# Attention stage of a fused kernel: the first inputs begun in order, the later ones as one transfer

## The chip, the cores and the metric

The kernel runs on one core of a Trainium2 chip. The metric is device time in microseconds (us) from launch to end; for one core it is the time of that core. The engines named below are TensorE (PE: matrix products, with PEld for its weight loads), VectorE (DVE), ScalarE (ACT), GpSimd (POOL) and SyncE (SP, which here only issues transfers, "DMA"s). ACT and POOL can issue transfers too. A transfer issued by SP stands in SP's queue, one issued by ACT in ACT's queue; sixteen DMA engines work off the packets of all queues. Shapes are written partitions x elements.

## The reference, cut to what matters

All arithmetic is in float32. The first half is a causal weighted sum over 7 neighbouring tokens for each of 8 heads, the second a mixture of experts in which each token goes to one expert by a greedy assignment with a capacity.

```python
B, S, D = 8, 3584, 192          # 28672 tokens; 8 heads of 24 columns, 7 weights each
w = softmax(weight, axis=-1)
x_pad = concat([zeros(B, 6, D), x], axis=1)
attn[b, s, h] = sum(w[h, k] * x_pad[b, s + k, h] for k in range(7))

logits = attn @ w_gate          # [28672, 8]
for idx in argsort(-logits.flatten()):      # greedy, capacity 3584 tokens an expert
    ...
out[mask_e] = relu(attn[mask_e] @ w1[e]) @ w2[e]        # 192 -> 1024 -> 192
```

## The kernel before, in words

**Two stages.** Stage 1 (from the start to about 164 us) computes `attn`, writes it to memory, and finds the assignment. Stage 2 (from there to the end) gathers each expert's tokens and applies its two matrices; there TensorE works nearly without a gap.

**Stage 1, tiles.** The 28672 tokens are 16 tiles (`NHB`) of 1792 tokens, two to a sequence. `load(i)` brings tile i into `X`, [118 partitions x 16 x 192]: 112 partitions (`W`) each hold one token of 16 windows, and the 6 partitions ahead of them, the halo, hold the 6 tokens before each window. So a load is a small transfer for the halo (line 189 in even tiles, 192 in odd ones) and two transfers of half of the 112 partitions' data each (line 194, windows 0 to 7 and 8 to 15). The first half is issued by SP, the second by ACT; for tile 0 both are issued by SP.

**conv(i)** takes one matrix product per head: `TH` (the 7 weights laid out as a 118 x 112 band, made by `toeplitz`) times X, in four PE instructions a head, into the PSUM tile `cv`; ACT then copies `cv` into the output tile `a` (an "evacuation"). `mid(h)`, called between the product and its evacuation, does other work: transposes of the previous tile's `a` (`aT`, DVE), the gate products (`pl`, `pt` on PE, with the gate matrix `GF`, which is the tile named `c_mu`), and steps of the assignment (`bg`), whose pace is set by a hand-kept model of engine time. After the eighth head ACT issues the store of `a` to `attn` (line 208, 1344 KB). For tile 14 the store is held back until head 2 of tile 15 (line 1631).

**What sets the order.** Each engine works its instructions in the order in which the program writes them. X has four buffers, so `load(i + 3)`, written ahead of `conv(i)`, waits until the PE instructions of `conv(i - 1)` are over; `a` has three buffers. `cv` has four. In the main loop (`for i in range(NHB)`) SP's issues are therefore halo, first half of tile i + 3, once a tile, and ACT's issues are the second half of tile i + 3 ahead of the eight evacuations of tile i, and the store behind them. Each transfer of SP and ACT reports on one of eight completion semaphores (DMAHW0 to DMAHW7), taken in turn; an engine that issues a transfer first waits until the transfer that used the same semaphore last has landed.

**The start.** `load(0)`, then `toeplitz`, in which `load(1)` stands behind the exponential, then `gate_ops`: four transfers of the gate matrix into the four 32-partition quarters of `wgr` (line 169), POOL's clearing of `GF` and its four copies of `wgr` into it (line 173), and two small DVE instructions on `pi`, made from a POOL instruction that stands behind those copies. Then `load(2)`, then the loop with `load(3)`.

**The end of stage 1.** At tile 13 the program issues the raw weights of the first expert (`wload`, lines 1229 to 1234, tiles `raw`) on SP, behind the load of tile 15. Inside `conv(13)` ACT rounds four of them to the type that the products of stage 2 need (`w<-raw`), each between two evacuations.

Of the kernel before, what the change touches and what calls it, by code (L numbers as in the profile page):

```python
# [6 lines left out]
F32 = mybir.dt.float32  # L7
# [8 lines left out]
NE, D, NTOK, F, CAP = 8, 192, 28672, 1024, 3584  # L16
W, HW_, NHB = 112, 16, 16
# [97 lines left out]
def build(ctx, tc, nc, x, weight, wg, attn, LT, wk):  # L115

    k = K()
    k.nc = nc
    k.tc = tc
    V, A, PE, P = nc.vector, nc.scalar, nc.tensor, nc.gpsimd  # L120
    cst = ctx.enter_context(tc.tile_pool(name="cst", bufs=1, side="right"))


    wb = cst.tile([128, 8, 7], F32, name="wb")
    nc.sync.dma_start(wb, bass.AP(tensor=weight.tensor, offset=weight.offset, ap=[[0, 128], [7, 8], [1, 7]]))
    pmi = cst.tile([128, 128], I32, name="pmi")
    P.iota(pmi, pattern=[[-1, 128]], base=0, channel_multiplier=1)
    D0 = cst.tile([128, 128], BF, name="D0")
    V.tensor_copy(D0, pmi)
    TH = cst.tile([128, 8, 128], F32, name="TH")  # L130
    P.memset(TH[:, :, W:128], 0.0)
    MK = cst.tile([128, 7, W], BF, name="MK")
    for j in range(7):
        V.tensor_scalar(MK[:, j], D0[:, 0:W], float(j), None, op0=OP.is_equal)
    wm = cst.tile([128, 8], F32, name="wm")

    def toeplitz():
        V.tensor_reduce(wm, wb, axis=AX.X, op=OP.max)
        V.tensor_tensor(wb, wb, wm[:, :, None].to_broadcast([128, 8, 7]), op=OP.subtract)
        A.activation(wb, wb, AF.Exp)  # L140
        load(1)
        V.tensor_reduce(wm, wb, axis=AX.X, op=OP.add)
        V.tensor_scalar(wm, wm, 1e-9, None, op0=OP.add)
        V.reciprocal(wm, wm)
        V.tensor_tensor(wb, wb, wm[:, :, None].to_broadcast([128, 8, 7]), op=OP.mult)

        tk = cst.tile([128, 2, W], F32, name="tk")
        for h in (1, 5):
            A.activation(TH[:, h, 0:W], MK[:, 0], AF.Copy, scale=wb[:, h, 0:1])
            for j in range(1, 7):  # L150
                A.activation(tk[:, j % 2], MK[:, j], AF.Copy, scale=wb[:, h, j:j + 1])
                P.tensor_tensor(TH[:, h, 0:W], TH[:, h, 0:W], tk[:, j % 2], op=OP.add)
        for hs in ((0, 2), (3, 4), (6, 7)):
            for j in range(7):
                for h in hs:
                    t = TH[:, h, 0:W]
                    if j == 0:
                        V.tensor_scalar(t, MK[:, 0], wb[:, h, 0:1], None, op0=OP.mult)
                    else:
                        V.scalar_tensor_tensor(t, MK[:, j], wb[:, h, j:j + 1], t, op0=OP.mult, op1=OP.add)  # L160


    wgr = cst.tile([128, 6, 8], F32, name="wgr")
    GF = wk.tile([128, 6, 32], F32, name="c_mu")
    pm = wk.tile([128, 1], F32, name="pm")

    def gate_ops():
        for pb in range(4):
            nc.sync.dma_start(wgr[32 * pb:32 * pb + 32], wg.rearrange("(c f) e -> f c e", f=32))
        P.memset(GF, 0.0)  # L170
        for pb in range(4):
            q = slice(32 * pb, 32 * pb + 32)
            P.tensor_copy(GF[q, :, 8 * pb:8 * pb + 8], wgr[q])

        pi = cst.tile([128, 1], I32, name="pi")
        P.iota(pi, pattern=[[0, 1]], base=0, channel_multiplier=1)
        V.tensor_scalar(pi, pi, 24, None, op0=OP.bitwise_and)
        V.tensor_scalar(pm, pi, 24.0, -1.0, op0=OP.is_equal, op1=OP.mult)


    X, AT, AA = {}, {}, {}

    def load(i):
        t = X[i] = k.xp[i % 4].tile([118, 16, D], F32, name="X")
        b, hf = divmod(i, 2)
        o = x.offset + (b * 3584 + hf * 1792) * D
        if hf == 0:
            P.memset(t[0:6, 0], 0.0)
            nc.sync.dma_start(t[0:6, 1:16], bass.AP(tensor=x.tensor, offset=o + (W - 6) * D,
                                                    ap=[[D, 6], [W * D, 15], [1, D]]))  # L190
        else:
            nc.sync.dma_start(t[0:6], bass.AP(tensor=x.tensor, offset=o - 6 * D, ap=[[D, 6], [W * D, 16], [1, D]]))
        for eng, w in ((nc.sync, 0), (A if i else nc.sync, 8)):
            eng.dma_start(t[6:118, w:w + 8], bass.AP(tensor=x.tensor, offset=o + w * W * D, ap=[[D, W], [W * D, 8], [1, D]]))

    def conv(i, mid, hold=None):
        t = X.pop(i)
        a = AA[i] = k.ap[i % 3].tile([128, 16, D], F32, name="a")
        o = a.rearrange("p w (h c) -> p h w c", c=24)
        for h in range(8):  # L200
            ps = k.cps.tile([128, 512], F32, name="cv")
            PE.matmul(ps[:, 0:384], TH[0:118, h], t[:, :, h * 24:(h + 1) * 24], start=True, stop=True)
            mid(h)
            A.activation(o[:, h], ps[:, 0:384].rearrange("p (w c) -> p w c", c=24), AF.Copy)
        put = partial(A.dma_start, attn[i * 1792:(i + 1) * 1792].rearrange("(g p b) d -> p g (b d)", g=4, b=4),
                      a[0:W].rearrange("p (g b) d -> p g (b d)", b=4))
        if hold is None:
            put()
        else:
            hold.append(put)  # L210

    def transp(i, u):

        if u == 0:
            AT[i] = [k.hp[i % 2].tile([128, 16, 6, 32], F32, name="aT")]
        V.transpose(AT[i][0][:, 4 * u:4 * u + 4].rearrange("p w c t -> p (w c t)"),
                    AA[i][:, 4 * u:4 * u + 4].rearrange("p w d -> p (w d)"))
        if u == 3:
            AA.pop(i)

    def logits(i, u):

        if u == 0:
            AT[i].append(k.bank("pl"))
        pl = AT[i][-1]
        for c in range(4):
            w = slice(4 * c, 4 * c + 4)
            PE.matmul(pl[32 * c:32 * c + 32, 0:128], GF[:, u], AT[i][0][:, w, u], start=(u == 0), stop=(u == 5))
        if u == 5:
            L = AT[i] = k.lrow()  # L230
            l, m = (t.rearrange("p (w t) -> p w t", t=32) for t in (L, pl[:, 0:128]))
            A.activation(l[:, :, 0:16], m[:, :, 0:16], AF.Copy)
            A.activation(l[:, :, 16:32], m[:, :, 16:32], AF.Identity, bias=pm)

    def logits_t(i):
        L = AT.pop(i)
        pt = k.bank("pt")
        PE.transpose(pt[:, 0:128], L, k.ident)
        v = pt[:, 0:128].rearrange("p (b q e) -> p e b q", q=4, e=8)
        o = LT[:, :, 16 * i:16 * i + 16].rearrange("p e (b q) -> p e b q", q=4)  # L240
        A.activation(o, v, AF.Copy)

    k.load, k.conv, k.transp, k.logits, k.logits_t = load, conv, transp, logits, logits_t
    k.toeplitz, k.gate_ops = toeplitz, gate_ops
    return k


# [1246 lines left out]
def moe_kernel(ctx, tc, x, weight, wg, w1, w2, out):  # L1494
# [6 lines left out]
    with ExitStack() as cw:  # L1501
# [110 lines left out]
        def hook(at):  # L1612
            nc.pe = max(nc.pe, PERIOD * at / 8 + START)
            bg.hook(1.5)
            if not got and len(bg.gens) == 3:
                first()
                got.append(at)

        split = partial(ff.wsplit, -1, V)
        more = [partial(k.transp, 12, 0), split, partial(k.transp, 12, 1), split, partial(k.transp, 12, 2), split,  # L1620
                partial(k.transp, 12, 3), split]
# [9 lines left out]
        last[15, 2].append(lambda: held.pop()())  # L1631
        del todo[:]
        k.load(0)
        k.toeplitz()
        k.gate_ops()
        k.load(2)
        r.consts()
        for i in range(NHB):
            if i + 3 < NHB:
                k.load(i + 3)  # L1640
            if i == 4:
                r.consts_late()
            if i == 13:
                cx[0].close()
                for _ in range(4):
                    ff.wload()
                ff.wpool(cw, 0, **late)

            def mid(h):

                if r.made:
                    d = nc.dve
                    for _ in range(2):
                        if more:
                            more.pop(0)()
                    nc.dve = d
                for f in last.get((i, h), ()):
                    f()
                if i and h == 0 and i < LAG:
                    for u in range(4):  # L1660
                        left.append(partial(k.transp, i - 1, u))
                        if i > 1:
                            left.append(partial(gate, i - 2, u) if u < 3 else partial(end, i - 2))
                if left:
                    left.pop(0)()
                hook(8 * i + h)

            k.conv(i, mid, held if i == 14 else None)
# [88 lines left out]
```

## Time and profile before

| what | value |
|---|---|
| time, median of 3 runs (lowest to highest) | 1237.59 us (1235.33 to 1238.16) |
| time of the profiled execution | 1247.95 us |
| its span | 1246.2 us |
| its mean granted TensorE clock | 0.993 |
| busy: PE, DVE, ACT, POOL | 1208.1 us (97%), 983.6 us (79%), 560.8 us (45%), 535.4 us (43%) |
| first product of stage 2 (`ph`) | 163.6 us after the span's start |

The profile follows one execution, which took 10.36 us longer than the median of the timed runs; its span leaves out 1.75 us around the work. The page has the span in 40 slices (31 us each): the first slice is the start, slices 1 to 4 are tiles 2 to 15, and from slice 5 on it is stage 2. "DMA share" in a table by stretches is the busy share of the 16 DMA engines; records overlap a little, so that a full stretch reads 1.05 to 1.11. In a timeline a row is one instruction, or several of a kind in a row (x4); the time ahead of it is its start, the second its length, and in brackets stand the idle time ahead of it and what ended it. Rows of queues (SPq, ACTq) start when the engine came to the issue; a wait that stands there is part of the row's length or of the gap ahead of it.

### The profile page before, as it was taken

Reading aid. Unit: us, or ns where it says so; the run is one execution under the profiler, and the core shown is the slowest. Engines: PE = TensorE matmul, PEld = TensorE weight load, DVE = VectorE, ACT = ScalarE, POOL = GpSimd, SP = SyncE. Lnnn points to the kernel's source line nnn. Section 1 sums busy time; section 2 is a strip of 40 time slices with the busy share of each in tenths; the row PEclk is TensorE's granted clock in tenths of the full one; section 3 lists DMA queues with packets and bytes.
Section 4 is the critical chain, followed back from the end, with each engine's and each line's share of the span. In section 5 each row is a group of like instructions: output and inputs, shape, how many; then the busy total and the mean of one; then the engine's idle time right before and its main releaser. Section 6 shows DMA issues by size and latency. Waiting matters only on the chain.

```text
span 1246.2 us, 21782 instructions
## 1 busy us (share of the span) xinstructions
PE 1208.1 (97%) x7694; PEld 1036.6 (83%) x7694; DVE 983.6 (79%) x2122; ACT 560.8 (45%) x1251; POOL 535.4 (43%) x524
## 2 busy tenths in 40 slices
PE   5999899999999999999999999999999999999997
PEld 2445578889989898889888889999999999999997
DVE  7388778988898988889889866777777777777772
ACT  4454455556435554445544443333333333343332
POOL 3000233535455554555465445445434544444522
PEclk9999999999999999999999999999999999999999
DMA  9999664569526473746343442114233222413100
GB/s 242 332 338 321 216 220 123 147 156 305 170 85 176 156 229 110 246 132 216 102 132 98 128 106 73 38 46 158 72 118 107 96 98 96 158 58 136 48 23 28
DMA packets 129220, 182.02 MB, mean 146 GB/s; under 512 B 21632, under 2 KB 91728, under 8 KB 127440
## 3 DMA queue, kind: packets, MB, share of 16 engines
q1 hardware_dynamic: 86496, 104.15, 27.5%
q0 software_dynamic: 21504, 44.07, 11.9%
q10 hardware_dynamic: 21104, 32.34, 7.9%
q8 instruction: 62, 1.02, 0.3%
q14 instruction: 54, 0.44, 0.1%
HBM read 102.38 MB, written 78.12 MB: 145 GB/s over the span
## 4 chain that ended last, share of the span: by engine, by line
PE 83%; DVE 6%; DMA 5%; issue 2%; ACT 1%; SPq 1%; another core or an unknown queue 0%; POOL 0%; POOLq 0%; ACTq 0%; DVEq 0%
PE ph L56 39%; PE y L56 38%; DMA X<-in_x_dram 4%; PE cv L56 2%; PE bg L56 2%; DVE X L56 1%; DVE aT L56 1%; DMA attn<-a 1%; DVE hl L56 1%; PE pl L56 1%; DMA raw<-in_moe_w_dram 1%; PE px L56 0%; DVE yo L56 0%; SPq L569 0%
## 5 line engine op out<-in xcount | busy, mean ns | idle before, releaser
L56 PE MATMUL y<-w,hh 128*128 128x384 f32 x1792 | 535.6, 355 | 0.0
L56 ACT ACTIVATE hh<-ph 128x512 fp32r<-128x512 f32 x448 | 267.7, 598 | 451.1 <-PE ph L56 389.6
L56 PE MATMUL y<-w,hl 128*128 128x192 f32 x1792 | 448.9, 251 | 0.0
L56 DVE SCALAR_TENSOR_TENSOR hl<-ph,hh 128x512 fp32r<-128x512 f32 x448 | 307.8, 687 | 128.7 <-ACT hh L56 101.4
L56 PE MATMUL ph<-xa,w 128*128 128x512 f32 x1344 | 395.2, 402 | 0.2 <-DVE hl L56 0.2
L56 PEld LDWEIGHTS y<-w,hl 128*128 128x128 f32 x1792 | 340.9, 190 | 16.2
L56 PEld LDWEIGHTS y<-w,hh 128*128 128x128 f32 x1792 | 336.3, 188 | 20.9 <-issue 2.9
L1377 POOL DMA_INDIRECT out_dram<-yo,ia x128 | 145.3, 1135 | 236.8 <-DVE yo L56 194.0
L56 PEld LDWEIGHTS ph<-xa,w 128*128 128x128 f32 x1344 | 218.4, 189 | 21.4 <-issue 1.6
L1377 POOL DMA_INDIRECT out_dram<-yo,ib x96 | 95.2, 991 | 220.5 <-DVE yo L56 213.1
L56 PE MATMUL ph<-xd,w 128*128 128x512 f32 x448 | 177.4, 396 | 0.0
L1302 POOL DMA_INDIRECT xg<-attn,ja x128 | 141.3, 1104 | 80.8 <-issue 39.2
L56 PE MATMUL ph<-xd,dl 128*128 128x512 f32 x448 | 174.2, 389 | 0.2 <-issue 0.2
L56 DVE STREAM_TRANSPOSE xs<-xg 32x128 f32<-32x128 f32 (+2 forms) x408 | 164.8, 404 | 6.6
L56 ACT ACTIVATE yt<-y 128x192 f32<-128x192 f32 x224 | 73.1, 326 | 111.5 <-PE y L56 71.8
L56 PE MATMUL cv<-X,TH 118*128 118x384 f32 x256 | 104.5, 536 | 17.7 <-DVE TH L56 11.4
L56 DVE TENSOR_TENSOR yo<-y,yt 128x192 f32<-128x192 f32 x224 | 79.2, 354 | 49.6 <-ACT yt L56 46.0
L1302 POOL DMA_INDIRECT xg<-attn,jb x96 | 103.6, 1079 | 29.3 <-issue 29.3
L56 PEld LDWEIGHTS ph<-xd,dl 128*128 128x128 f32 x448 | 84.2, 188 | 20.2 <-issue 0.5
L56 PEld LDWEIGHTS ph<-xd,w 128*128 128x128 f32 x448 | 84.0, 187 | 19.7 <-issue 0.6
L56 PEld LDWEIGHTS cv<-X,TH 118*128 118x128 f32 x256 | 46.7, 203 | 50.0 <-issue 15.0
L56 ACT ACTIVATE a<-cv 128x384 f32<-128x384 f32 x128 | 59.7, 492 | 50.0 <-PE cv L56 26.9
(237 smaller groups left out, 920.2 us busy)
## 6 DMA issues: line engine op xcount, KB each, us to landing
attn<-a ACTq DMA_DIRECT2D x16, 1344.0 KB
X<-in_x_dram SPq DMA_DIRECT2D x17, 672.0 KB
raw<-in_moe_w_dram SPq DMA_DIRECT2D x56, 192.0 KB
X<-in_x_dram ACTq DMA_DIRECT2D x15, 672.0 KB
kw<-w SPq DMA_DIRECT2D x36, 256.0 KB
kv<-w SPq DMA_DIRECT2D x24, 384.0 KB
scr<-xs SPq DMA_DIRECT2D x96, 96.0 KB
w<-kw SPq DMA_DIRECT2D x6, 1536.0 KB
```

Source lines behind the costliest of these rows:

```text
L56: return f(*a, **k)
L1302: self.nc.gpsimd.indirect_dma_start(out=t[:, b], out_offset=None, in_=self.attn[0:rows], in_offset=bass.IndirectOffsetOnAxis(ap=idx[b], ax ...
L1377: st = self.nc.gpsimd.indirect_dma_start(out=self.out, out_offset=bass.IndirectOffsetOnAxis(ap=idx, axis=0), in_=o, in_offset=None, bounds ...
```

## The change

- `load` gets a second argument. With it (tiles 1, 2 and 3) the first half is issued by SP and the second is put on a list, `later`, from which ACT issues it at a place of its own: tile 1 where `load(1)` stood in `toeplitz`, tile 2 behind `toeplitz`, tile 3 inside `conv(0)` at head 4, which is behind four evacuations. Without it (tile 0, and 4 to 15) all 112 partitions x 16 windows go as one transfer of 1344 KB on SP. From tile 4 on, ACT issues stores only.
- SP's order at the start becomes tile 0, tile 1, gate matrix, tile 2, tile 3.
- The gate matrix is one transfer into 32 partitions; its four copies into `GF` are DVE's instead of POOL's.

```diff
-    def toeplitz():
+    def toeplitz(more):
...
-        load(1)
+        more.pop(0)()
...
-    wgr = cst.tile([128, 6, 8], F32, name="wgr")
+    wgr = cst.tile([32, 6, 8], F32, name="wgr")
...
+    def gate_load():
+        nc.sync.dma_start(wgr, wg.rearrange("(c f) e -> f c e", f=32))
+
     def gate_ops():
-        for pb in range(4):
-            nc.sync.dma_start(wgr[32 * pb:32 * pb + 32], wg.rearrange("(c f) e -> f c e", f=32))
         P.memset(GF, 0.0)
         for pb in range(4):
-            q = slice(32 * pb, 32 * pb + 32)
-            P.tensor_copy(GF[q, :, 8 * pb:8 * pb + 8], wgr[q])
+            V.tensor_copy(GF[32 * pb:32 * pb + 32, :, 8 * pb:8 * pb + 8], wgr)
...
-    def load(i):
+    def load(i, later=None):
...
-        for eng, w in ((nc.sync, 0), (A if i else nc.sync, 8)):
-            eng.dma_start(t[6:118, w:w + 8], bass.AP(tensor=x.tensor, offset=o + w * W * D, ap=[[D, W], [W * D, 8], [1, D]]))
+        def part(eng, w, n):
+            eng.dma_start(t[6:118, w:w + n], bass.AP(tensor=x.tensor, offset=o + w * W * D, ap=[[D, W], [W * D, n], [1, D]]))
+
+        if later is None:
+            part(nc.sync, 0, 16)
+        else:
+            part(nc.sync, 0, 8)
+            later.append(partial(part, A, 8, 8))
...
         k.load(0)
-        k.toeplitz()
+        k.load(1, later)
+        k.gate_load()
+        k.load(2, later)
+        k.toeplitz(later)
+        later.pop()()
         k.gate_ops()
-        k.load(2)
         r.consts()
         for i in range(NHB):
             if i + 3 < NHB:
-                k.load(i + 3)
+                k.load(i + 3, None if i else later)
...
+                if i == 0 and h == 4:
+                    later.pop()()
```

The three places in the order of instructions that the prediction speaks of follow. The words in brackets are the semaphores for which the instruction waits.

SP at the start, before. Numbered names: X_180 is tile 0, X_188 tile 1, X_278 tile 2, X_312 tile 3.

```order
L189 DMA X_180<-in_x_dram 6x15x192
L194 DMA X_180<-in_x_dram 112x8x192 x2
L192 DMA X_188<-in_x_dram 6x16x192
L194 DMA X_188<-in_x_dram 112x8x192
L169 DMA wgr_141<-in_moe_w_gate_dram 32x6x8 [waits DMAHW0_49]
L169 DMA wgr_141<-in_moe_w_gate_dram 32x6x8 [waits DMAHW1_49]
L169 DMA wgr_141<-in_moe_w_gate_dram 32x6x8 [waits DMAHW2_49]
L169 DMA wgr_141<-in_moe_w_gate_dram 32x6x8 [waits DMAHW3_49]
L189 DMA X_278<-in_x_dram 6x15x192 [waits DMAHW5_49]
L194 DMA X_278<-in_x_dram 112x8x192 [waits DMAHW6_49]
```

The same of the change; here X_180 is tile 0, X_184 tile 1, X_188 tile 2, X_308 tile 3.

```order
L189 DMA X_180<-in_x_dram 6x15x192
L194 DMA X_180<-in_x_dram 112x16x192
L192 DMA X_184<-in_x_dram 6x16x192
L194 DMA X_184<-in_x_dram 112x8x192
L168 DMA wgr_141<-in_moe_w_gate_dram 32x6x8
L189 DMA X_188<-in_x_dram 6x15x192 [waits DMAHW0_49]
L194 DMA X_188<-in_x_dram 112x8x192 [waits DMAHW2_49]
L192 DMA X_308<-in_x_dram 6x16x192 [waits DMAHW3_49]
L194 DMA X_308<-in_x_dram 112x8x192 [waits DMAHW5_49]
```

Tile 2's load stood behind four transfers of the gate matrix, each of which waits for an earlier transfer to land; now it stands behind one that waits for none.

ACT in tiles 0 and 1, before: the issue of a second half of X (line 194) stands ahead of each tile's eight evacuations.

```order
L56 ACTIVATE a<-cv 128x16x24 [waits PE_49] x8
L208 DMA attn<-a 112x4x768 [waits DMAHW7_49,Activation_49]
L194 DMA X<-in_x_dram 112x8x192 [waits DMAHW3_49,DMAHW2_49,DMAHW1_49]
L56 ACTIVATE a<-cv 128x16x24 [waits PE_49] x8
L208 DMA attn<-a 112x4x768 [waits DMAHW5_49,Activation_49]
L194 DMA X<-in_x_dram 112x8x192 [waits DMAHW7_49,DMAHW6_49]
```

The same of the change, from tile 2's second half on (the store is line 214 there):

```order
L194 DMA X<-in_x_dram 112x8x192
L56 ACTIVATE a<-cv 128x16x24 [waits PE_49] x4
L194 DMA X<-in_x_dram 112x8x192 [waits DMAHW1_49]
L56 ACTIVATE a<-cv 128x16x24 [waits PE_49] x4
L214 DMA attn<-a 112x4x768 [waits DMAHW4_49,Activation_49]
L56 ACTIVATE a<-cv 128x16x24 [waits PE_49] x8
L214 DMA attn<-a 112x4x768 [waits DMAHW7_49,Activation_49]
```

Between two stores ACT issues no load any more, and no evacuation stands behind one that waits for a transfer, but for tile 3's.

SP at tile 15 (X_1238), before:

```order
L192 DMA X_1238<-in_x_dram 6x16x192 [waits DMAHW5_49,DMAHW0_49,PE_49]
L194 DMA X_1238<-in_x_dram 112x8x192 [waits DMAHW7_49]
L1229 DMA raw_1371<-in_moe_w1_dram 128x512 [waits DMAHW1_49]
L1231 DMA raw_1373<-in_moe_w1_dram 64x512 [waits DMAHW2_49]
```

The same of the change (tile 15 is X_1223):

```order
L192 DMA X_1223<-in_x_dram 6x16x192 [waits DMAHW7_49,PE_49]
L194 DMA X_1223<-in_x_dram 112x16x192 [waits DMAHW0_49]
L1235 DMA raw_1355<-in_moe_w1_dram 128x512 [waits DMAHW2_49]
L1237 DMA raw_1357<-in_moe_w1_dram 64x512 [waits DMAHW3_49]
```

The raw weights now follow 1344 KB of tile 15 in SP's queue, where 672 KB stood ahead of them.

More of the change, by code (lines that the diff above doesn't have):

```diff
@@ L243, in build @@
     k.load, k.conv, k.transp, k.logits, k.logits_t = load, conv, transp, logits, logits_t
-    k.toeplitz, k.gate_ops = toeplitz, gate_ops
+    k.toeplitz, k.gate_load, k.gate_ops = toeplitz, gate_load, gate_ops
     return k
@@ L1617, in hook @@
                 got.append(at)
+        later = []
         split = partial(ff.wsplit, -1, V)
```

## The prediction

> **What bounds the kernel now.** I read the page first, then the busy shares by stretches of stage 1, then the chain of waits and the timelines of SP, ACT and PE around the edits. The page (busy time of engines, and tenths of each 31 us slice):
>
> ```profile
> PE 1208.1 (97%) x7694; PEld 1036.6 (83%) x7694; DVE 983.6 (79%) x2122; ACT 560.8 (45%) x1251; POOL 535.4 (43%) x524
> PE   5999899999999999999999999999999999999997
> ```
>
> TensorE is the bound from end to end, and only the first slice and the fifth (124 to 156 us) have room worth speaking of. Work is moved in stage 1 alone, so the end moves by as much as stage 2's first product does. The stretches of stage 1 (start:end, length, busy time of PE, PEld, DVE, ACT, POOL with their instructions, granted clock, DMA share, GB/s):
>
> ```profile
> 3.50:24.00 20.50, 12.57 (x29) 6.74 (x30) 17.67 (x59) 11.30 (x28) 9.99 (x34) 1.00 1.11 240
> 48.00:72.00 24.00, 22.90 (x198) 12.03 (x197) 15.06 (x32) 12.58 (x34) 0.25 (x1) 1.00 1.06 334
> 72.00:97.00 25.00, 24.03 (x202) 12.48 (x201) 23.76 (x63) 13.07 (x34) 0.50 (x2) 1.00 1.07 326
> 129.00:160.00 31.00, 26.64 (x267) 17.09 (x266) 18.73 (x39) 14.71 (x37) 9.01 (x9) 0.89 0.57 179
> ```
>
> Until tile 13 the DMA engines are full (share above 1): 240 GB/s while they only load, some 330 with loads and stores. The issues of one tile are these:
>
> ```profile
> attn<-a ACTq DMA_DIRECT2D x16, 1344.0 KB
> X<-in_x_dram SPq DMA_DIRECT2D x17, 672.0 KB
> X<-in_x_dram SPq DMA_DIRECT2D x8, 72.0 KB
> 48.49 0.27 SPq L192 DMA_DIRECT2D X<-in_x_dram  x1
> 56.49 0.27 SPq L189 DMA_DIRECT2D X<-in_x_dram  x1
> 116.74 0.27 SPq L192 DMA_DIRECT2D X<-in_x_dram  x1
> ```
>
> A store of 1344 KB, two halves of 672 KB (the second is ACT's) and a halo of some 70 KB are 2.82 MB, at 334 GB/s 8.5 us a tile. The halo of a tile is issued when the conv of four tiles earlier frees its buffer, so these rows pace the tiles: tile 7 to tile 15 are 68.25 us, 8.53 a tile. One tile alone shows 8.00 (48.49 to 56.49). So one tile's chain can do 8.0 and the transfers need 8.5. From 72 on VectorE is nearly full too (23.76 of 25.00).
>
> **The start.** The timelines of PE and of SP (start, length, rows with the idle time and its releaser in brackets), then ACT's:
>
> ```profile
> 5.00 6.31 SPq L169 DMA_DIRECT2D wgr<-in_moe_w_gate_dram  x4
> 17.24 0.31 SPq L194 DMA_DIRECT2D X<-in_x_dram  x1
> 18.57 6.69 PE L56 MATMUL cv<-X,TH 118*128 118x384 f32 x20 [0.22 <-DVE TH L56]
> 28.24 2.90 PE L56 MATMUL cv<-X,TH 118*128 118x384 f32 x4 [2.98 <-DMA X<-in_x_dram]
> 38.77 1.45 PE L56 MATMUL cv<-X,TH 118*128 118x384 f32 x4
> 48.41 1.46 PE L56 MATMUL cv<-X,TH 118*128 118x384 f32 x4
> ```
>
> ```profile
> 31.93 0.87 ACT L56 ACTIVATE a<-cv 128x384 f32<-128x384 f32 x2 [6.15 <-DMA X<-in_x_dram]
> 44.30 2.02 ACT L56 ACTIVATE a<-cv 128x384 f32<-128x384 f32 x5 [4.68 <-DMA X<-in_x_dram]
> ```
>
> conv(2) starts at 28.24, 2.98 us late, since tile 2's first half was issued at 17.24, behind four gate-matrix issues that waited for landings (5.00 to 11.31, and the halo behind them). conv(3) starts 10.53 later and conv(4) another 9.64, against 8.0: ACT stood at its X issues for 6.15 and 4.68 us with finished products unevacuated.
>
> **What the change removes here.** Tile 2's first half waits only for tile 0, whose last part had landed when the last gate transfer was issued, about 11. Ahead of it then stand tiles 0 and 1, and with it goes tile 2's other half: three tiles are 4.34 MB, at 240 GB/s 18.1 us from 3.5, so 21.6; if tile 3's half shares the engines, 24.5 (another 0.69 MB). Both lie ahead of 25.26, where conv(1)'s products end (18.57 + 6.69). So the 2.98 us go, less 0.13 for a normal changeover: **2.85 us**. With ACT no longer issuing loads, conv(2) and conv(3) can take 8.0 each: 10.53 + 9.64 - 16.0 = **4.2 us**. Together conv(4) may start 7.0 us earlier, at 41.4.
>
> **What of it is given back.** conv(5) and conv(6) need loads 5 and 6:
>
> ```profile
> 31.54 20.25 DMA X<-in_x_dram
> 56.37 1.45 PE L56 MATMUL cv<-X,TH 118*128 118x384 f32 x4
> 59.82 0.31 SPq L194 DMA_DIRECT2D X<-in_x_dram  x1
> 63.96 1.45 PE L56 MATMUL cv<-X,TH 118*128 118x384 f32 x4
> ```
>
> Load 5's first half landed at 51.79 (31.54 + 20.25, in the chain of waits), 4.6 ahead of its conv at 56.37. Line 194 at 59.82 waited for a landing of tile 6, 4.1 ahead of conv(6) at 63.96. Full engines can't bring loads earlier than their bytes allow, so the lead is capped near **4.4 us** at tile 5. From there to tile 12 it has no loads against it. The chain of waits runs through VectorE there:
>
> ```profile
> 88.99 0.93 DVE X L56 x3
> 89.92 0.90 DVE aT L56
> ```
>
> and this work only follows the tiles. So I expect some 4 us of lead at tile 12, between 0.3 (8.5 - 8.0 over 8 tiles takes 4.1) and 4.4. What it is worth is settled at tile 13, by bytes.
>
> The 20.25 us are long for 672 KB. The Trainium skill ("DMA: Bandwidth & Descriptors", section "Why a DMA increments its semaphore by 16 and not by 1") says that a transfer goes to the largest number of engines, up to 16, that divides its outer dimension, so that a 6-partition halo would load six engines and those would lag; by it load 5's lag stays with the change, as no halo is altered, and the cap too; the trace shows the length (20.25) and not the engines.
>
> **The small edits.** Rows of POOL and DVE:
>
> ```profile
> 17.62 1.97 POOL L173 COPY c_mu<-wgr 32x48 f32<-32x48 f32 x4 [4.91 <-DMA wgr<-in_moe_w_gate_dram]
> 19.83 0.15 DVE L56 TENSOR_SCALAR pi<-pi 128x1 int32<-128x1 int32 x1 [1.16 <-POOL pi L176]
> ```
>
> DVE takes over four copies of 32x48, which POOL did in 1.97 us. They stand where DVE waited 1.16 us for POOL anyway; the nearest DVE row is 0.15 for a 128x1, so they cost 0.6 to 2.0 us of DVE, in the 9.6 us between TH's end (18.57) and conv(2). The gate products need them first in tile 2. Nothing, with that cover; without it, at most 2.0 once. Three gate transfers less (6 KB each) are nothing.
>
> **The late loss.** SP around tile 15, ACT in conv(13), and the chain there:
>
> ```profile
> 117.41 0.79 SPq L1229 DMA_DIRECT2D raw<-in_moe_w_dram  x1
> 118.32 13.02 DMA attn<-a
> 131.35 6.02 DMA raw<-in_moe_w_dram
> 129.68 0.32 ACTq L208 DMA_DIRECT2D attn<-a  x1
> 131.28 0.65 ACT L56 ACTIVATE w<-raw 128x512 fp32r<-128x512 f32 x1
> 135.18 0.51 ACT L56 ACTIVATE a<-cv 128x384 f32<-128x384 f32 x1
> 137.45 0.63 ACT L56 ACTIVATE w<-raw 128x512 fp32r<-128x512 f32 x1 [1.76 <-DMA raw<-in_moe_w_dram]
> 138.51 0.91 PE L56 MATMUL cv<-X,TH 118*128 118x384 f32 x2 [0.64 <-ACT a L56]
> ```
>
> The four roundings of raw weights stand among conv(13)'s evacuations at fixed places. The first ran at 131.28, the last at 137.45, released by a transfer whose issue had waited for the store issued at 118.32 (to 131.34), and PE stood for an evacuation behind it at 138.51: this sets PE now. A lead in the tiles doesn't help it, as long as the engines are full of the same bytes.
>
> In the change the raws follow the whole of tile 15 in SP's queue: 0.69 MB more, 2.1 us at 334 GB/s, and the other half stands in no other queue. The store issued at 129.68 stood behind that half in ACT's queue; now nothing is ahead of it, and it can go ahead of the raws for up to its whole 4.1 us (1.38 MB at 334). So the first rounding falls at 131.28 + 2.1 - 1 (an issue earlier by part of the lead) = 132.4 at the least, and at 131.28 + 2.1 + 4.1 = 137.5 at the most. I take the middle, **135.0**: the two queues share. From the first to the fourth rounding ACT needs 4.4 us if no raw is late (131.28 to 135.69, where the evacuation ahead of the fourth ended). The fourth then falls at 136.8 to 141.9, by my value at 139.4, against 137.45: -0.6 to +4.4, I take **+2.0 us**. Four evacuations queue behind it in ACT, PE's products behind those (four `cv` buffers), and every conv, gate step and gather that follows is in order behind them. After such a wait the clock costs something:
>
> ```profile
> 28.00:37.00 9.00, 8.76 (x56) 4.31 (x60) 1.38 (x2) 2.35 (x5) 0.00 (x0) 0.65 1.06 375
> 145.00:160.00 15.00, 11.66 (x118) 6.99 (x117) 6.91 (x10) 4.62 (x14) 8.94 (x9) 0.77 0.29 85
> 151.29 0.48 PE L56 MATMUL pt<-ident,L 128*128 128x128 f32 x1 [3.34 <-ACT L L56]
> ```
>
> After PE's idle 2.98 us the clock of 28 to 37 is 0.65; after the 3.34 ahead of 151.29 that stretch has 0.77. Between nothing and a loss like the first's ((1 - 0.65) x 9 = 3 us) I take **1.0**: with conv(13) begun early, PE's wait for the first rounding is one of several microseconds, and part of the slow clock falls on ACT's waits.
>
> The Trainium skill ("DMA: Bandwidth & Descriptors", section "Queues, rings and completion order") says that on each engine descriptors are taken in the order of their queue and the queues are served in turn; by it the raws must wait for all of tile 15, as I have it, and the sum stays; the trace agrees so far as the raw issued at 117.41 was rounded only at 131.28.
>
> Sum: the early 7.0, capped at 4.4, end in a wait for the raws, worth nothing beyond it; +2.0 + 1.0 = **+3.0 us**. The profiled execution was 1247.95, so 1250.95 in a profile of like conditions; the median lies 10.36 lower, so 1237.59 + 3.0 = **1240.6 us**.
>
> **The rivals.**
>
> *Faster: the lead survives.* For it: with a lead of 4.4 the raws and the stores are issued that much earlier, and the raw that set the end no longer stands behind so late a store; if the engines find the time, the fourth rounding comes at 137.45 - 4.4 = 133.05. Against: a DMA share above 1 all the way. The end would move by 4 to 6 us (up to 7.0 without the cap), 1237.59 - 5 = **1232.6**.
>
> *No change: an absorbing wait.* The 3.34 us before 151.29, and 5.12 us of the chain at 145.71 that the profile puts down to an unknown queue, may swallow what conv(13) loses or gains, and the engines' bytes stay the same. The first rounding at its lower bound gives the same (-0.6). Then 1237.6 within 2.5 us. The Trainium skill ("DMA: Bandwidth & Descriptors", section "Issuing engines are not separate DMA queues") says that transfers of all issuing engines end up on the same 16 engines, so moving them saves issue time only; alone, that gives this rival.
>
> *Much slower: loads starve behind stores.* While a store runs almost alone the engines move more:
>
> ```profile
> 26.00:29.00 3.00, 0.76 (x1) 0.50 (x2) 3.00 (x4) 0.00 (x0) 0.00 (x0) 0.74 1.04 393
> ```
>
> If the queues are served in turn, and a store's pieces are larger than a load's, a store alone in its queue runs at 393 GB/s (1.38 MB, 3.5 us) and the loads, all in the other queue, then at 240 (1.45 MB, 6.0 us; some 0.4 of it during the store): 9.1 a tile against 8.53. Over tiles 5 to 15 that is 6.3 us, less the lead of 4.4, and the late loss on top: 6.3 - 4.4 + 3.0 = 4.9, or 9.3 where no lead is left: **1242.5 to 1246.9**. It decides from a tile pace of about 8.9. Against: before, at 48 to 72, loads and stores mix at 334 with the same bytes.
>
> *The change doesn't do what it says*: tile 2's second half stays behind ACT's building of TH, about 11.5, and if conv(2) still waited past 28, the early 2.85 would be gone; with conv(3)'s and conv(4)'s 4.2 left, about the capped lead, the time would be that of the forecast, 1240.6. It is in that chance.
>
> **How the numbers follow.** My forecast has 0.32, much slower 0.10, no change 0.28, faster 0.30. A measurement tells about 0.2% (2.5 us) from no change. So faster 0.30, same 0.28, slower 0.42. The forecast's own range, from -0.6 without a clock loss to +4.4 and 3.0, is 1237.0 to 1245.0. With most of the faster case (1237.59 - 6.6) and of the much slower one, 1231 to 1247 leaves out 2 in 10.
>
> **What would show it.** Right: conv(2) starts near 25.4, no evacuation in conv(2) to conv(4) is released by X, conv(6) starts 3 to 5 us earlier than 63.96; the first rounding of a raw weight at 134 to 136 and the fourth at 138.5 to 140.5. Wrong: a fourth rounding before 136 and a first `ph` before 161 (the lead survived); a halo pace above 8.9 (starving); a late conv(13), but `ph` at 163.6 (absorbed).

## The result and the profile after

The change made the kernel **slower: 1246.74 us against 1235.98 (medians of 7 runs each), ratio 1.0074, 95% interval 1.0052 to 1.0096**. A second comparison, on a chip where both take longer, gave 1255.13 against 1246.91, ratio 1.0059 (1.0039 to 1.0078). The forecast of 1240.6 had the side right; of the size (+9.1 us by the ratio, +10.8 by the medians) it had about a third.

One thing has to be known to read the two profiles side by side: chips differ. The kernel before took 1235 us on one chip of the experiments and 1247 on the two others, and its first profile (1247.95) reads like those taken on the other two, the change's (1240.44) like those taken on that one. The kernel before was therefore profiled once more on a chip where it takes 1235 us, and that execution (1235.01) stands beside the change's below. Its early part is the one already shown (conv(2) released by X at 28.90 there, 28.24 in the first); the 3.34 us ahead of 151.29 are missing.

The stretches of stage 1 of the kernel before, second profile (columns as above):

```profile
24.00:48.00 24.00, 19.59 (x134) 9.79 (x133) 8.73 (x11) 9.11 (x24) 1.79 (x3) 0.86 1.07 345
48.00:72.00 24.00, 22.99 (x198) 12.08 (x197) 15.09 (x32) 12.56 (x34) 0.25 (x1) 1.00 1.07 341
97.00:129.00 32.00, 30.48 (x300) 18.30 (x299) 27.58 (x50) 14.52 (x38) 1.99 (x3) 1.00 1.04 324
129.00:160.00 31.00, 30.41 (x342) 20.49 (x342) 22.27 (x45) 18.78 (x47) 10.17 (x11) 1.00 0.69 220
```

The same of the change:

```profile
24.00:48.00 24.00, 20.99 (x169) 10.90 (x171) 12.50 (x16) 12.22 (x31) 1.79 (x3) 1.00 1.06 349
48.00:72.00 24.00, 21.10 (x177) 10.75 (x169) 13.19 (x31) 12.12 (x31) 0.50 (x2) 1.00 1.03 314
97.00:129.00 32.00, 30.40 (x282) 17.87 (x283) 23.50 (x43) 12.15 (x31) 1.95 (x3) 0.89 1.04 303
129.00:160.00 31.00, 28.11 (x291) 18.08 (x292) 22.36 (x45) 17.81 (x46) 7.90 (x8) 1.00 0.72 217
```

The reader sees the gain in the first row (169 PE instructions against 134) and the loss in the next two: PE does less from 48 on, and the DMA engines, as busy as before (1.03 and 1.04), move 314 and 303 GB/s instead of 341 and 324.

PE's timeline in the change, at every conv that was released by X, and at the first product of stage 2:

```profile
33.55 1.45 PE L56 MATMUL cv<-X,TH 118*128 118x384 f32 x4
44.30 1.53 PE L56 MATMUL cv<-X,TH 118*128 118x384 f32 x4 [3.01 <-DMA X<-in_x_dram]
54.15 1.53 PE L56 MATMUL cv<-X,TH 118*128 118x384 f32 x4 [2.02 <-DMA X<-in_x_dram]
62.57 1.53 PE L56 MATMUL cv<-X,TH 118*128 118x384 f32 x4 [0.60 <-DMA X<-in_x_dram]
86.96 1.53 PE L56 MATMUL cv<-X,TH 118*128 118x384 f32 x4 [0.25 <-DMA X<-in_x_dram]
98.22 2.90 PE L56 MATMUL cv<-X,TH 118*128 118x384 f32 x4 [3.17 <-DMA X<-in_x_dram]
162.63 0.96 PE L56 MATMUL ph<-xa,w 128*128 128x512 f32 x3
```

These are conv(3), then conv(4), (5), (6), (9) and (10). conv(3) starts at 33.55 instead of 38.77 (39.49 in the second profile), so the start is won as forecast. From conv(4) on the loads hold the tiles back: five of the seven convs from conv(4) to conv(10) wait for X, and the six tiles from 44.30 to 98.22 take **8.99 us each**. In the second profile of the kernel before the same six, 48.47 to 97.03, take 8.09. Part of the difference is the lead being given back: conv(10) comes only 1.2 us later than before, after a conv(4) that came 4.2 earlier. The first product of stage 2 comes at 162.63; in the second profile of the kernel before:

```profile
157.48 0.96 PE L56 MATMUL ph<-xa,w 128*128 128x512 f32 x3
```

5.15 us later, out of the 5.43 us between the two executions (1240.44 and 1235.01): nearly all of it is made in stage 1. It is made in two places. conv(13) starts 2.6 us later than in the second profile of the kernel before:

```profile
130.34 0.81 PE L56 MATMUL cv<-X,TH 118*128 118x384 f32 x2
```

```profile
127.78 0.81 PE L56 MATMUL cv<-X,TH 118*128 118x384 f32 x2
```

The rest comes between there and `ph`. The profiled execution of the change is the shortest of its seven, so this profile shows only half of the loss by the medians. The other runs took 1242 to 1249 us; their mean clock is 0.990 to 0.994 where the profiled one has 0.995, so they probably have more half-clock stretches like the one behind 98.22, where four products took 2.90 us instead of 1.5. A second profile of the change that lies at its median stands with e7 below (c2).

SP's timeline in the change shows where the loads are held:

```profile
36.32 8.38 SPq L189 DMA_DIRECT2D X<-in_x_dram  x1
45.61 8.03 SPq L192 DMA_DIRECT2D X<-in_x_dram  x1
121.91 0.93 SPq L194 DMA_DIRECT2D X<-in_x_dram  x1
122.88 6.56 SPq L1235 DMA_DIRECT2D raw<-in_moe_w_dram  x1
```

A halo's issue, 0.27 us in most tiles before, takes 6 to 9 us up to tile 13: SP stands at it with tiles still under way in its queue. Tile 15 is issued at 121.91 (before, 117.06), and the first raw weight behind it is held another 6.56. That isn't the wait for its completion semaphore: the transfer that had used it last, a store, had landed at 121.47. ACT's timeline at the first and the fourth rounding, and the piece of the chain of waits ahead of the fourth:

```profile
137.94 0.63 ACT L56 ACTIVATE w<-raw 128x512 fp32r<-128x512 f32 x1 [3.96 <-DMA raw<-in_moe_w_dram]
142.84 0.63 ACT L56 ACTIVATE w<-raw 128x512 fp32r<-128x512 f32 x1 [0.49 <-DMA raw<-in_moe_w_dram]
```

```profile
132.24 10.52 DMA raw<-in_moe_w_dram
```

131.28 and 137.45 before (131.30 and 137.40 in the second profile): 6.7 and 5.4 us later.

### The profile page after: what moved, and what is told of

Read it like the earlier page. It is cut to its first block, busy times and chain, and to the rows that moved or that the text cites. A ratio compares the mean times of both kernels' runs of the same rounds, so it can differ in the third digit from the quotient of the medians.

```text
span 1238.7 us, 21749 instructions
## 1 busy us (share of the span) xinstructions
PE 1202.9 (97%) x7694; PEld 1034.1 (83%) x7694; DVE 985.3 (80%) x2126; ACT 567.0 (46%) x1251; POOL 531.6 (43%) x520
## 4 chain that ended last, share of the span: by engine, by line
PE 90%; DMA 4%; DVE 2%; SPq 2%; ACT 1%; issue 0%; POOL 0%; POOLq 0%; DVEq 0%; ACTq 0%
PE ph L56 42%; PE y L56 40%; PE cv L56 3%; DMA X<-in_x_dram 3%; PE bg L56 3%; SPq L189 1%; DVE TH L56 1%; PE pl L56 1%; DMA raw<-in_moe_w_dram 1%; SPq L1235 1%; PE px L56 0%; DVE X L56 0%; DMA wb<-in_weight_dram 0%; DVE aT L56 0%; SPq L194 0%
## 5 line engine op out<-in xcount | busy, mean ns | idle before, releaser
L56 PE MATMUL cv<-X,TH 118*128 118x384 f32 x256 | 102.0, 523 | 25.2 <-DVE TH L56 13.2
```

Source lines behind the costliest of these rows:

```text
L56: return f(*a, **k)
```

## The experiments

Each run stands beside the kernel before on the same chip. The theories: **A**, the later inputs come too slowly, and **Q**, they do because all loads stand in one queue and the stores alone in the other; **B**, the start costs; **C**, only the raw weights behind tile 15 cost; later **H**, the six halo engines, and **S**, the size of a transfer.

| run | chip | this, us | before, us | ratio (95% interval) |
|---|---|---|---|---|
| e1 start only | 13 | 1232.29 | 1234.95 | 0.9979 (0.9970 to 0.9988) |
| e2 later inputs only | 13 | 1250.35 | 1234.95 | 1.0131 (1.0116 to 1.0147) |
| e3 two halves on SP | 13 | 1241.86 | 1234.95 | 1.0057 (1.0041 to 1.0072) |
| b2 kernel before again | 13 | 1235.01 (one) | 1234.95 | |
| e5 no halos | 12 | 1251.67 | 1247.62 | 1.0026 (1.0016 to 1.0037) |
| e6 tiles alternate | 12 | 1248.83 | 1247.62 | 1.0006 (0.9995 to 1.0017) |
| e7 raws ahead of tile 15 | 12 | 1250.59 | 1247.62 | 1.0016 (0.9999 to 1.0032) |
| e8 halves on ACT, mid-tile | 12 | 1243.49 | 1247.62 | 0.9956 (0.9942 to 0.9969) |
| c2 the change again | 10 | 1255.13 | 1246.91 | 1.0059 (1.0039 to 1.0078) |
| e7 again | 10 | 1247.20 | 1246.91 | 0.9993 (0.9977 to 1.0010) |
| e1 again | 10 | 1244.61 | 1246.91 | 0.9970 (0.9955 to 0.9984) |
| e8 again | 10 | 1241.98 | 1246.91 | 0.9954 (0.9936 to 0.9972) |

### e1: the start alone

```diff
-        if later is None:
+        if i == 0:
             part(nc.sync, 0, 16)
+        elif later is None:
+            part(nc.sync, 0, 8)
+            part(A, 8, 8)
```

> Only the first part of the change: tiles 0 to 3 and the gate matrix begun in order as in the change, but from tile 4 on each input comes as before, half on SP and half on ACT. Theory A (the loss is made by the later inputs, which as one transfer each on SP come at a pace of some 9.0 us a tile instead of 8.5): the pace from tile 5 to tile 12 is that of before, no conv waits for X there, and some of the early lead of 4 to 5 us is kept: 1230 to 1235 us against 1236. Theory B (the loss is made at the start, by the new order or the gate matrix): slower than before by 5 us or more, as the whole change. Theory C (the loss is only at tile 13, raw weights behind the whole of tile 15): the first rounding of a raw weight near 131 as before, time as in A.

2.7 us faster. The start is a gain, not a loss (B falls), and with the later loads in two queues no conv of it is released by X. Its first rounding ran at 129.53 and `ph` at 154.41, 3.07 us ahead of the kernel before. Of the 7.0 us that the prediction gave conv(4), 3.1 are there (45.37 against 48.47 in the second profile); ACT stands at its issues again:

```profile
26.55 4.14 PE L56 MATMUL cv<-X,TH 118*128 118x384 f32 x12 [2.92 <-ACT a L56]
41.80 1.56 PE L56 MATMUL cv<-X,TH 118*128 118x384 f32 x4 [0.89 <-ACT a L56]
50.95 1.56 PE L56 MATMUL cv<-X,TH 118*128 118x384 f32 x4 [1.49 <-ACT a L56]
```

### e2: the later inputs alone

```diff
-        for eng, w in ((nc.sync, 0), (A if i else nc.sync, 8)):
+        for eng, w, n in (((nc.sync, 0, 8), (A if i else nc.sync, 8, 8)) if i < 4 else ((nc.sync, 0, 16),)):
```

> Only the second part: the start as before, tiles 0 to 3 in halves, from tile 4 on one transfer of 1344 KB on SP. Theory A: all of the loss, and more than the whole change's 9 us, since there is no early lead to pay from: pace 8.9 to 9.1 us a tile, convs from tile 6 on waiting for X, 1245 to 1252 us. Theory B: no loss, 1236 within 3 us. Theory C: the pace stays at 8.5 to 8.6 and no conv before 13 waits for X; the first rounding at 134 to 138, 1238 to 1243 us.

15.4 us slower, more than the whole change: all of the loss is here, and in the whole change the early lead pays part of it. Four short stretches of this kernel, two while a store runs and two while loads run alone (columns as above):

```profile
52.50:55.50 3.00, 3.00 (x25) 1.68 (x17) 0.59 (x2) 1.96 (x6) 0.25 (x1) 1.00 1.03 401
57.00:60.00 3.00, 3.00 (x27) 1.35 (x29) 1.84 (x3) 1.47 (x3) 0.00 (x0) 1.00 1.07 229
62.00:64.50 2.50, 2.50 (x24) 1.36 (x23) 1.91 (x7) 1.53 (x4) 0.00 (x0) 1.00 1.04 406
70.50:73.50 3.00, 0.64 (x3) 0.39 (x3) 2.93 (x6) 0.66 (x2) 0.25 (x1) 1.00 1.11 238
```

The same stretches of e1, where each queue holds loads:

```profile
52.50:55.50 3.00, 3.00 (x26) 1.81 (x25) 0.47 (x2) 1.96 (x6) 0.25 (x1) 1.00 1.08 359
57.00:60.00 3.00, 3.00 (x24) 1.34 (x22) 1.97 (x3) 2.06 (x5) 0.00 (x0) 1.00 1.07 314
62.00:64.50 2.50, 2.50 (x24) 1.35 (x23) 1.78 (x6) 0.70 (x3) 0.00 (x0) 1.00 1.07 385
70.50:73.50 3.00, 2.99 (x25) 1.43 (x24) 2.93 (x6) 0.95 (x3) 0.25 (x1) 1.00 1.05 330
```

With the queues split by kind the engines swing between 400 and 230 GB/s in these stretches; by the packets of the trace, the stores move 346 and 336 GB/s in the first and third and the loads beside them 50 and 72, and then the loads, nearly by themselves, 224 and 226. With loads in both, the rate stays between 314 and 385. The engines are busy either way (share 1.03 to 1.11); what a busy engine moves is not the same. e2's edit also joins two transfers into one, so it does not tell the queue from the size; e3 does.

### e3: two transfers of 672 KB, both on SP

```diff
-        if later is None:
+        if i == 0:
             part(nc.sync, 0, 16)
+        elif later is None:
+            part(nc.sync, 0, 8)
+            part(nc.sync, 8, 8)
```

> The whole change, but from tile 4 on an input comes as two transfers of 672 KB, both on SP. It tells the size of a transfer from the queue it stands in. If it is the queue (all loads in one queue, stores alone in the other): pace 8.9 to 9.1 as in the change, 1243 to 1250 us. If it is the size of a transfer (a conv waits for the whole of it, SP's issue is held until a larger one is through): the pace falls back toward 8.5, 1234 to 1240 us.

1.0057, and 9.6 us more than e1 on the same chip (1241.86 against 1232.29), from which it differs only in the queue of the second halves; so the queue alone makes a loss, with transfers no larger than before. The rate at which the engines move bytes is lower with it too. In this order, e3 and e1:

```profile
48.00:72.00 24.00, 22.90 (x186) 11.89 (x179) 12.58 (x31) 12.05 (x31) 0.50 (x2) 0.96 1.04 308
48.00:72.00 24.00, 21.57 (x179) 11.14 (x178) 14.72 (x34) 12.05 (x33) 0.50 (x2) 1.00 1.07 362
```

But the tiles hardly pay for it here. conv(4) to conv(10), 44.47 to 96.81, take 8.72 a tile, between the two cases (e1: 8.34). Two convs wait for X (conv(4), and conv(10) at 96.81), and conv(13) starts at 126.11, as in e1 (126.02). The raws are as late as in the change (the first rounding at 139.03, in e1 at 129.53), and PE stands behind them:

```profile
140.57 1.65 PE L56 MATMUL cv<-X,TH 118*128 118x384 f32 x2 [6.91 <-ACT a L56]
```

`ph` comes at 164.04, 9.63 us after e1's. So all that e3 loses to e1 it loses between conv(13) and `ph`, where the raw weights are late. Whether whole tiles of 1344 KB slow the pace further was not told apart from the early waits and the half clock of the change's profile.

### b2: the kernel before once more

> The kernel before once more, for a second profiled execution. The first one took 1247.95 us against a median of 1236, with 3.34 us of idle TensorE ahead of 151.29 and half its clock behind it. If these belong to that one execution, they are missing here, the first product of stage 2 starts at 156 to 160 instead of 163.6, and the execution takes 1234 to 1240 us. If they belong to the kernel, all is as in the first profile.

As the first case said: `ph` at 157.48, no 3.34 us. The edit is none. The same kernel on chips 10 and 12 takes 12 us more, and all but one of the profiles taken there have a wait of PE of 2.5 to 2.7 us between 144 and 159 us, put down to "issue", which those of chip 13 lack. Its cause was not sought.

### e5: no halos

```diff
-        if hf == 0:
+        if i > 3:
+            P.memset(t[0:6], 0.0)
+        elif hf == 0:
```

> The whole change without the halo transfers of tiles 4 to 15 (GpSimd clears those 6 partitions instead, so the 6 tokens ahead of each window are left out of the sums of those tiles). In the change the loads come every 9.0 us and a load's last landing lies some 7 us behind the typical one. Theory H (the six engines that take the halos set the pace): without them the pace falls to 8.4 or less, SP's issues are no longer held for 6 to 9 us, no conv waits for X: 1232 to 1237 us. Theory Q (all loads stand in one queue and the stores alone in the other, so that a store runs at some 350 GB/s with the loads nearly stopped and the loads then run alone at 220 to 250): 70 of 2760 KB a tile are little, the pace stays at 8.7 to 9.0, 1240 to 1247 us.

PE's timeline (conv(6) and conv(9)):

```profile
60.40 1.91 PE L56 MATMUL cv<-X,TH 118*128 118x384 f32 x4 [1.80 <-DMA X<-in_x_dram]
87.42 1.53 PE L56 MATMUL cv<-X,TH 118*128 118x384 f32 x4 [0.84 <-DMA X<-in_x_dram]
```

conv(9) starts at 87.42 where the change has 86.96, and conv(10) at 98.67 against 98.22: without halos the loads come no faster. H falls as a cause of the pace. (The three tiles shown take 9.01 us each, but over these three the change took 8.13; the waits fall on other tiles.) The waits begin a tile later, and 1.0026 is less than c2's 1.0059, but those two ran on different chips, so what halos cost is left open.

### e6: odd tiles on ACT, even ones on SP

```diff
-            part(nc.sync, 0, 16)
+            part(A if i % 2 and i > 3 else nc.sync, 0, 16)
```

> The whole change, but the one transfer of an odd tile from 5 on is issued by ACT, that of an even tile by SP; the halos stay on SP. Theory Q: with loads in both queues a store shares its queue with a load again, the pace goes back to about 8.5, and the first rounding of a raw weight to about 131, as tile 15 is in ACT's queue: 1231 to 1237 us, though ACT's evacuations may wait for its own issue. Theory S (the size of 1344 KB counts, not the queue): pace near 9.0, 1243 to 1248 us.

1.0006, no difference. The halo rows of SP's timeline:

```profile
56.94 0.27 SPq L189 DMA_DIRECT2D X<-in_x_dram  x1
89.25 0.27 SPq L189 DMA_DIRECT2D X<-in_x_dram  x1
```

Four tiles in 32.31 us, 8.08 each, and no conv but conv(4) waits for X. That agrees with Q but does not show it: from conv(5) to conv(9) the change itself took 8.20 a tile, conv(4) comes 2.9 us later here, so that less lead could be lost, and the rate is not that of the kernel before (299 GB/s from 72 to 97, at a share of 1.08, against 336). Tile 15, an odd one, is also in ACT's queue, so the raw weights don't stand behind it; the first rounding comes at 133.50. conv(4) pays for all of the start: tile 4 and tile 5 then come side by side in two queues, and both have landed only at 46.8 and 48.2.

```profile
47.17 2.90 PE L56 MATMUL cv<-X,TH 118*128 118x384 f32 x4 [6.08 <-DMA X<-in_x_dram]
```

### e7: raw weights ahead of tile 15

```diff
+            if i == 12:
+                for _ in range(4):
+                    ff.wload()
             if i + 3 < NHB:
                 k.load(i + 3, None if i else later)
...
             if i == 13:
-                for _ in range(4):
-                    ff.wload()
```

> The whole change, but the raw weights of the first expert are issued on SP ahead of tile 15's load instead of behind it. It prices the part of the loss that the forecast put there. If all of the change's loss lies at tile 13: back to 1233 to 1237 us, the first rounding no longer waits. If the pace of the loads is the greater part: roundings on time, but conv(15) waits for a tile 15 that comes later by the raws' 0.79 MB (2 to 4 us), and convs 4 to 10 wait for X as in the change: 1240 to 1246 us.

> The change itself, on the same chip as the three runs beside it, since the chips differ by 12 us for the kernel before. The pace of the loads and the waits for X should be as in the first profile of the change (convs 4, 5 and some later ones wait for X, first rounding of a raw weight at 136 to 139): ratio 1.005 to 1.010.

> The change with the raw weights issued ahead of tile 15, beside the change on one chip. If the wait for the raws at tile 13 is the greater part of the loss, it is 5 us or more faster than the change beside it; if the pace of the loads is, it is 0 to 4 us faster and still slower than before by 0.2 to 0.6%.

On chip 10, 1247.20 beside the change's 1255.13: **7.9 us of the loss go with this one edit**, and what is left equals the kernel before. That is the first of the two cases. On chip 12 e7 was at 1.0016 of the kernel before (0.9999 to 1.0032); the change was not run there. The same move in the kernel before was not tried; there, only the fourth rounding waited for a raw, 1.26 us in the second profile. The pace itself stayed slow, and convs still waited for X. PE's timeline of e7 on chip 10:

```profile
43.47 1.53 PE L56 MATMUL cv<-X,TH 118*128 118x384 f32 x4 [2.82 <-DMA X<-in_x_dram]
81.17 1.53 PE L56 MATMUL cv<-X,TH 118*128 118x384 f32 x4 [3.06 <-DMA X<-in_x_dram]
117.76 1.53 PE L56 MATMUL cv<-X,TH 118*128 118x384 f32 x4 [0.43 <-DMA X<-in_x_dram]
127.96 0.81 PE L56 MATMUL cv<-X,TH 118*128 118x384 f32 x2
162.18 0.96 PE L56 MATMUL ph<-xa,w 128*128 128x512 f32 x3
```

conv(4) to conv(12), eight tiles at 9.29 (8.64 in the second profile of the kernel before). Beside it, PE's timeline of the change on the same chip:

```profile
43.98 2.90 PE L56 MATMUL cv<-X,TH 118*128 118x384 f32 x4 [3.09 <-DMA X<-in_x_dram]
129.05 0.81 PE L56 MATMUL cv<-X,TH 118*128 118x384 f32 x2
142.40 1.65 PE L56 MATMUL cv<-X,TH 118*128 118x384 f32 x2 [5.79 <-ACT a L56]
169.79 0.96 PE L56 MATMUL ph<-xa,w 128*128 128x512 f32 x3
```

and its ACT timeline:

```profile
140.85 0.63 ACT L56 ACTIVATE w<-raw 128x512 fp32r<-128x512 f32 x1 [8.16 <-DMA raw<-in_moe_w_dram]
```

The change again (c2) has no edit. The slow pace eats the early lead, roughly even: conv(13) starts at 129.05 in c2 and 127.96 in e7, against 127.33 and 127.78 in the two profiles of the kernel before. The raws behind tile 15 then stop ACT for 8.16 us and PE for 5.79, and the granted clock from 129 to 160 is 0.88 where e7 has 0.94. So 1.1 us between the two at conv(13) become 7.6 at `ph`, and that reaches the end. In e7 the first rounding ran at 134.18.

### e8: halves in both queues, ACT's behind four evacuations

```diff
-                k.load(i + 3, None if i else later)
+                k.load(i + 3, later)
...
-                if i == 0 and h == 4:
+                if later and h == 4:
```

> The start of the change, and for every later tile the first half on SP and the second on ACT, as before, but issued behind four evacuations of the running conv instead of ahead of all eight. Theory Q gives the pace of before (8.5). ACT then should hold fewer finished products back at its issue than with the issue ahead of the conv (there PE waited 2.92, 0.89 and 1.49 us for evacuations in tiles 2 to 5): 1229 to 1233 us against 1232.3. If the later second halves make convs wait for X instead: 1233 to 1238 us.

> The start of the change alone (later inputs in halves on SP and ACT as before, the ACT half ahead of the conv), to stand beside the next run: ratio 0.997 to 0.9985 as measured already.

> The same with ACT's half behind four evacuations. On the other chip its ratio was 0.9956. If the later issue on ACT is worth something in itself, it is 2 to 4 us faster than the run before it on this chip; if the difference was only the chip's, the two agree within 1 us.

0.9956 and 0.9954 on two chips; on chip 10 that is **4.9 us faster than the kernel before, 13.2 than the change** (1241.98 against 1246.91 and 1255.13). Beside e1 on chip 10 it is 2.6 us ahead. `ph` starts at 154.94 there, against 162.00 in e1 and 169.79 in the change; e1's profiled execution took 1249.16, 4.6 more than its median, so the first distance is too wide. This is the version to keep.

## Why the prediction was right, and where it failed

The side was forecast with its mechanism, raw weights that come late behind the whole of tile 15. The size was not: 1246.74 lies above the forecast's own range (1237.0 to 1245.0) and only 0.3 us inside the outer one (1231 to 1247). That it lies inside at all is luck rather than insight, as the upper end comes from a rival that was given 0.10.

**The start** held. conv(3) was forecast to end about 41.4 with conv(4) free to start; its last products ended at 41.2 (39.63 + 1.56). The lead was capped at about 4.4; conv(4) started at 44.30, 4.1 us ahead of 48.41. But the cap came a tile earlier than I put it: load 4, which I had not worked out, held conv(4) 3.01 us.

**"From there to tile 12 it has no loads against it"** is the step that failed. Convs 5, 6, 9 and 10 waited for loads, conv(6) came 1.4 us early instead of 3 to 5, and conv(10) 1.2 late. In the sum the lead was worth nothing past the raws, so this step spoiled the forecast through two terms of the late loss: tile 15's issue, put 1 us earlier, and the rate of 334 GB/s. I had priced this mechanism as the rival "loads starve behind stores", at 9.1 us a tile, with 8.9 as the point from which it decides, and given it 0.10. It measured 8.99 from conv(4) to conv(10), and e2 showed the swing that the rival described (401 and 229 GB/s against its 393 and 240). The halo rows, which were to be the sign, don't tell: tile 7 to tile 15 is 9.27 a tile by their starts (45.61 to 119.73), but 8.53, as before, by their ends (53.64 to 121.86). What I held against it, that loads and stores mix at 334 GB/s with the same bytes, was a mix of loads in *both* queues, and the change takes just that away. The rival's times, 1242.5 to 1246.9, hold the 1246.74, but with another split: it put 6.3 on the pace and 3.0 on the raws, and by e7 the raws are worth 7.9 of the 8.2 us on chip 10, while the pace costs about what the start had won.

**The late loss** was the right place and mechanism, with the size off. Terms: the first rounding at 135.0 (132.4 to 137.5) measured 137.94 and, on chip 10, 140.85; the fourth at 139.4 measured 142.84. I had taken tile 15's issue 1 us earlier because of the lead. It came 4.9 later (121.91 against 117.06), since SP's issues were held, and the raws' own issue was held 6.56 more. The +2.0 was +5.4 by the fourth rounding, and by e7 this part is worth 7.9 us with its half clock, where the forecast had +3.0. The clock's term, +1.0, can't be told from the rest.

**The rivals.** "The lead survives" is ruled out for the change, though e1 and e8 show that it survives once the later loads stay in two queues (-2.7 and -4.9 us). "An absorbing wait" did not absorb: `ph` moved with the fourth rounding (5.4 us and 5.15). Part of what was to absorb it, the 3.34 us, is missing in the second profile of the kernel before.

**Small edits.** They are part of e1 and e8, which are faster; alone they were not tried. One count above is wrong: the page has 256 products `cv` for 16 tiles of 8 heads, so a head takes two PE instructions, not four; no sum used it.

**The Trainium skill.** Its page "DMA: Bandwidth & Descriptors", section "Issuing engines are not separate DMA queues", says that issuing on several engines saves only the time of issuing. Here the measurement differs: the same bytes, with half of each load moved from ACT's queue to SP's, cost 9.6 us (e3 beside e1), and the engines, as busy, moved 308 GB/s instead of 362 from 48 to 72. The section "Queues, rings and completion order" of that page, where an engine goes round the queues packet by packet, agrees with the swing in e2.

## What to carry to other kernels

When loads are moved to a queue of their own, ask what the other queue then holds: where it held only stores here, the loads fell to 50 to 72 GB/s during a store and ran at about 225 after it, and the average fell although the engines looked just as full. A DMA share above 1 says that engines are busy, not how much they move; read the GB/s beside it, stretch by stretch. And whoever makes a transfer longer should look at what is queued behind it that someone waits for: here four small weight loads behind the last input carried most of the loss (7.9 of 8.2 us on chip 10).

## What the runs showed of the hardware that I had not expected

- **The mix of queues sets the rate of busy engines**: 229 to 238 GB/s for loads in one queue, 401 to 406 while a store runs beside them, 314 to 385 with loads in both queues (e2 and e1, four stretches each); from 48 to 72, 308 with all loads on SP and 362 with halves in both queues (e3 and e1).
- **An issue can be held by its own queue**: with whole tiles on SP, halo issues took 6 to 9 us (8.38 at 36.32) where 0.27 was usual, and the first raw weight's issue 6.56 though its semaphore had been reached 1.4 us before. That the queue is full then is likely, but its room was not measured.
- **Chips differ by 1%**: the kernel before took 1234.95 us on chip 13, 1247.62 on 12 and 1246.91 on 10, while the ratios of e8 agree on 12 and 10 to 0.0002. Only comparisons on one chip tell a change of a few us.
